# Moving the first loads and splits of the second batch earlier, in a kernel of clustered attention followed by a gated feed-forward block

## The chip, the cores and the metric

One core of one Trainium2 chip. The metric is the device time of one execution in microseconds (us). Executions can fall into a fast or a slow state. The profile and the trace are of one execution each, taken by the hardware profiler; a profiled span is some 2 us shorter than the timed execution (347.4 against 349.2 us for the kernel before).

## The reference, cut to what matters

```python
def _attn_ref(q, k, v, centroids):           # q, k, v: 4 batches x 8 heads x 768 x 64
    q_n, k_n, c_n = ...                      # each row divided by its norm
    q_assign = np.argmax(np.einsum('bhsd,hcd->bhsc', q_n, c_n), axis=-1)   # 16 clusters
    k_assign = np.argmax(np.einsum('bhsd,hcd->bhsc', k_n, c_n), axis=-1)
    mask = q_assign[:, :, :, None] == k_assign[:, :, None, :]
    scores = scale * np.matmul(q, k.transpose(0, 1, 3, 2))
    scores = np.where(mask, scores, -1000000000.0)
    ...                                      # softmax
    return np.matmul(attn, v)

def _moe_ref(x, w_gate, w_val, w_out):       # x: 3072 x 512, d_ff 1536
    gate = 1.0 / (1.0 + np.exp(-(x @ w_gate)))
    return gate * (x @ w_val) @ w_out
```

The kernel adds the mask inside the score matmul: keys and queries are split into two fp16 halves (high and low), turned so that the 64 features lie on partitions 0 to 63, and 16 "mask rows" (the one-hot cluster of each position) are placed on partitions 64 to 79.

## The kernel before: the parts that matter

Work is laid out in steps, one score matmul and one exponential each, 24 steps for a pair of heads, 96 for a batch. `at(i, f)` puts a piece of background work behind the score matmul of step i. All engines are given their instructions in this order; SyncE, which issues most of the transfers, too.

```python
    def run_bg(i):
        for f in bg.pop(i, []):
            f()
    # ... in run_steps, for each step:
                do_scores(s)
                ...
                run_bg(step_no[0])
                step_no[0] += 1
```

A pair of the batches 1 to 3 is prepared by `pair_prep`. `use` is its first step; in what follows a pair is named by it (pair 96 is the first of the second batch). The four pairs of the first batch are called 0 to 3. `load` and `hop` are transfers that SyncE issues, and a hop copies mask rows into place.

```python
    def pair_prep(b, p, use, s0, gap):
        # ...
        def ot():                             # turn the mask of the pair
            st["ot"] = ohp.tile([128, NCH, 128], HP, tag="ohT", name="ohT")
            if use == 96:
                ps = oh_turn_pe(st["oh"], NCH)
                DVE.tensor_copy(st["ot"].rearrange("p c t -> p (c t)"), ps)
            else:
                SP.dma_start_transpose(out=st["ot"], in_=st["oh"].rearrange("p c x -> p (c x)"))
        # ...
        lead = 12
        for e in range(2):                    # two heads
            s = s0 + gap * e
            at(s, lambda e=e: sp(e, 0))                       # split the keys
            at(s + gap // 2 - 1, lambda e=e: sp(e, 1))        # split the queries
            at(s + gap - 1, lambda e=e: turn((b, 2 * p + e), st["hl", e], tp))   # DMA transpose
            at(s + gap + lead, lambda e=e: lgt(e))            # logits against the centroids
            # ... the clusters are picked in the three steps after
        s = s0 + 2 * gap + lead + 4
        at(s, ot)
        s += 1 if use == 96 else 10
        at(s, lambda: hops(0))                # copy the mask rows into place
        at(s + 1, lambda: hops(1))

    for b in range(1, B):
        for p in range(NP):
            use = 96 * b + 24 * p
            first = {96: (45, 54, 5), 120: (50, 68, 8), 144: (62, 84, 10)}
            ld, s0, gap = first.get(use, (use - 76, use - 58, 10))
            for side in ("k", "q", "v"):
                at(ld, lambda b=b, p=p, side=side: load(SP, side, b, p))
            pair_prep(b, p, use, s0, gap)
```

So a load is at step `ld`, the two transposes of a pair at s0 + gap - 1 and s0 + 2 gap - 1, the logits that read them 13 steps after each.

The softmax here doesn't subtract the row's maximum and nothing guards it: scores larger than these inputs give would overflow.

## Time and profile before

| kernel before | value | how to read it |
|---|---|---|
| time | 349.66 us | median of 2 runs, 349.44 to 349.88 |
| profiled span | 347.4 us | of which TensorE busy 326.6 us (94%) |
| idle time of TensorE | 20.8 us | the span less the busy time; 16.7 of it lies before 80 us, by the sums over windows |
| step 96 (second batch begins) | 71.51 us | the 97th score matmul in the timeline |
| step 112 | 82.10 us | feed-forward matmuls are mixed in from step 104 |

What the waits and chains look like stands in the prediction below.

### The profile page before, as it was taken

The numbers are of one execution on the slowest core, as the hardware profiler recorded it, in microseconds if no ns is written. First come the engines' busy times: TensorE is split into PE (matmuls) and PEld (weight loads), VectorE is DVE, ScalarE is ACT, GpSimd is POOL, SyncE is SP. The second block draws the span as 40 slices with busy tenths as digits, with TensorE's granted clock in tenths as the row PEclk, the third lists the DMA queues.
The fourth block names the chain that finished last, engine by engine and source line by source line (L and its number), as shares of the span: only waits on it lengthen the run. The fifth ranks groups of instructions, "written<-read, shape, count | busy, mean of one in ns | idle before, by whom it ended". The sixth has DMA issues, their size and how long they took to land.

```text
span 347.4 us, 8525 instructions
## 1 busy us (share of the span) xinstructions
PE 326.6 (94%) x3274; PEld 203.9 (59%) x3274; DVE 161.2 (46%) x384; ACT 232.0 (67%) x534; POOL 134.6 (39%) x221
## 2 busy tenths in 40 slices
PE   7898783899999999999999999999999999999995
PEld 3476562556665666566666665566665665565552
DVE  6467472475653556245544455444634232242230
ACT  5687793698886788678877786588876883332321
POOL 2994584264555464515464646445220000000000
PEclk9999996599999999999999999999999999999999
DMA  7999998496965397587466397533403111200102
GB/s 223 330 198 212 251 239 208 95 229 137 173 194 111 99 221 203 111 151 191 101 185 150 113 209 172 127 90 62 87 17 103 36 22 25 90 0 32 60 0 91
DMA packets 80999, 46.43 MB, mean 134 GB/s; under 512 B 60832, under 2 KB 77888, under 8 KB 80960
## 3 DMA queue, kind: packets, MB, share of 16 engines
q1 hardware_dynamic: 76960, 40.99, 48.4%
q0 software_dynamic: 3712, 4.72, 8.0%
q8 instruction: 25, 0.41, 0.5%
q10 hardware_dynamic: 288, 0.20, 0.2%
q14 instruction: 14, 0.11, 0.1%
HBM read 28.34 MB, written 6.29 MB: 100 GB/s over the span
## 4 chain that ended last, share of the span: by engine, by line
PE 85%; DMA 7%; DVE 3%; ACT 3%; SPq 1%; issue 1%; POOL 0%; DVEq 0%
PE g L343 18%; PE v L358 18%; PE o L375 18%; PE sc L469 16%; PE av L486 9%; DMA T<-hl 3%; PE lg L275 2%; DMA qraw<-in_q_dram 2%; ACT es L474 2%; DMA T<-ohT 1%; PE t_ps L597 1%; PE lg L612 1%; PE oh_ps L325 1%; DVE hT L363 0%; PE wm L560 0%
## 5 line engine op out<-in xcount | busy, mean ns | idle before, releaser
L474 ACT ACTIVATE es<-sc 128x384 f16<-128x384 f32 x384 | 173.4, 497 | 44.0 <-PE sc L469 32.2
L469 PE MATMUL sc<-T 80*128 80x384 f16 (+1 forms) x384 | 119.2, 333 | 4.6 <-DMA T<-ohT 2.2
L486 PEld LDWEIGHTS <-es 128*128 128x128 f16 x1152 | 83.4, 99 | 46.0 <-issue 3.1
L363 DVE SCALAR_TENSOR_TENSOR hT<-th,v 128x384 f16<-128x384 f32 x96 | 53.1, 553 | 101.2 <-PE av L486 66.9
L486 PE MATMUL av<-va,es 128*128 128x65 f16 x1152 | 99.3, 195 | 0.2
L343 PE MATMUL g<-xTb,wg 128*128 128x384 f16 x384 | 78.2, 325 | 0.6 <-DVE xTb L510 0.2
L358 PE MATMUL v<-xTb,wv 128*128 128x384 f16 x384 | 78.1, 325 | 0.1
L239 POOL TENSOR_TENSOR xp<-t,rec 128x384 f16<-128x384 f32 x31 | 25.8, 831 | 129.1 <-DVE rec L238 123.1
L375 PE MATMUL o<-wo,hT 128*128 128x512 f16 x288 | 70.6, 379 | 0.0
L349 ACT ACTIVATE th<-g 128x384 f32<-128x384 f32 x96 | 47.2, 492 | 27.5 <-DVE hT L363 16.2
L343 PEld LDWEIGHTS <-wg 128*128 128x128 f16 x384 | 37.3, 97 | 22.5 <-issue 1.3
L358 PEld LDWEIGHTS <-wv 128*128 128x128 f16 x384 | 37.3, 97 | 21.1 <-issue 0.5
L375 PEld LDWEIGHTS <-hT 128*128 128x128 f16 x288 | 27.9, 97 | 25.5
L469 PEld LDWEIGHTS <-T 80*128 80x128 f16 (+1 forms) x384 | 37.6, 98 | 4.8 <-DMA T<-ohT 2.9
L384 ACT ACTIVATE ob<-o 128x512 f32<-128x512 f32 x16 | 9.6, 597 | 22.2 <-PE o L375 22.2
L237 DVE TENSOR_TENSOR t<-av,sv 128x390 f32<-128x390 f32 x32 | 18.0, 561 | 13.6 <-PE av L486 13.3
L746 POOL TENSOR_TENSOR hl<-qraw,hl 128x384 f16<-128x384 f32 x24 | 22.0, 915 | 4.8 <-DVE hl L745 3.3
L746 POOL TENSOR_TENSOR hl<-kraw,hl 128x384 f16<-128x384 f32 x24 | 22.5, 939 | 2.8 <-PE sc L469 1.2
L196 DVE TENSOR_REDUCE vs<-vraw 128x64 f16<-128x384 f32 x24 | 19.2, 814 | 0.0
L275 PE MATMUL lg<-cm,T 128*128 128x32 f16 x288 | 11.0, 177 | 8.0 <-DMA T<-hl 8.0
L281 ACT COPY lglo<-lg 128x192 f32<-128x192 f32 x24 | 7.7, 321 | 13.0 <-PE lg L275 13.0
L382 DVE TENSOR_SCALAR ob<-o 128x512 f32<-128x512 f32 x8 | 5.5, 692 | 22.8 <-PE o L375 22.8
(83 smaller groups left out, 216.6 us busy)
## 6 DMA issues: line engine op xcount, KB each, us to landing
vraw<-in_v_dram SPq DMA_DIRECT2D x16, 384.0 KB, 5.3
out_dram<-ob SPq DMA_DIRECT2D x24, 256.0 KB, 2.3
kraw<-in_k_dram SPq DMA_DIRECT2D x15, 384.0 KB, 3.5
qraw<-in_q_dram SPq DMA_DIRECT2D x15, 384.0 KB, 4.5
wg<-in_moe_w_gate_dram POOLq DMA_DIRECT2D x2, 768.0 KB, 10.3
wv<-in_moe_w_val_dram POOLq DMA_DIRECT2D x2, 768.0 KB, 13.2
wo<-in_moe_w_out_dram POOLq DMA_DIRECT2D x4, 384.0 KB, 15.3
T<-ohT SPq DMA_DIRECT2D x58, 24.0 KB, 1.9
```

What stands on the lines that cost most here:

```text
L196: DVE.tensor_reduce(s[:, e, 0:64], RAW["v", b, p][:, e].rearrange("p c d -> p d c"), AX.X, ALU.add)
L237: DVE.tensor_tensor(t, av, sv, ALU.add)
L239: eng.tensor_tensor(x, t[..., 0:64], bcast(r, 64), ALU.mult)
L343: PE.matmul(out=g[:, 0:n], lhsT=wg[fc // WQ][:, dc, fc % WQ, :], rhs=xT[:, dc, t0 : t0 + n], start=(dc == 0), stop=(dc == NDC - 1),)
L349: ACT.activation(th[:, 0:n], g[:, 0:n], AF.Tanh, scale=0.5)
L358: PE.matmul(out=w[:, 0:n], lhsT=wv[fc // WQ][:, dc, fc % WQ, :], rhs=xT[:, dc, t0 : t0 + n], start=(dc == 0), stop=(dc == NDC - 1),)
L363: DVE.scalar_tensor_tensor(hT[:, fc, 0:n], st[0][:, 0:n], 1.0, w[:, 0:n], ALU.add, ALU.mult)
L375: PE.matmul(out=o, lhsT=hT[:, fc, bass.ts(t, 128)], rhs=wo[fc // 3][:, fc % 3, :], start=(fc == 0), stop=(fc == NFC - 1),)
L469: PE.matmul(out=sc.rearrange("p (c t) -> p c t", t=128), lhsT=s["k"], rhs=s["q"], start=True, stop=True,)
L474: ACT.activation(es, sc, AF.Exp, scale=SCALE)
L486: PE.matmul(out=av[:, s["c0"] + i, :], lhsT=s["es"][:, bass.ts(i, 128)], rhs=VA[b, p][:, e, s["j"], :], start=(first and i == 0), stop=(la ...
L746: POOL.tensor_tensor(hl[:, :, 64:128], r, hl[:, :, 0:64], ALU.subtract)
```

## The change

Its intent: have the second batch's first pairs loaded, split and turned earlier, so that TensorE does not wait for their transposes around 50 to 62 us; bring the turns of the first batch's third pair forward for the same reason; and take two query casts and some warm-up matmuls off the path to the first score. The whole diff:

```diff
--- before.py
+++ after.py
@@ -512,7 +512,7 @@
         if last_x:
             at(step_no[0] + 5, by_pe)
         elif b == 0:
-            at(47 + 4 * p, by_dma)
+            at(49 + 3 * p, by_dma)
         else:
             by_dma()
 
@@ -695,14 +695,14 @@
     for e in range(2):
         split(e, 9, 12, ACT, POOL)
     k_split(1)
+    dummies(1)
+    first_pick(0)
+    first_place(0)
     for e in range(2):
         split(2 + e, 6, 12, ACT, POOL)
     load_w(0)
     dummies(3)
-    first_pick(0)
-    first_place(0)
-    dummies(3)
-    for s in range(8):
+    for s in range(4):
         at(s, lambda: dummies(1))
     for s, f in (
         (0, lambda: turn_pe([(1, 0, 6)], DVE)),
@@ -723,13 +723,13 @@
         if p > 1:
             at(U - 38, lambda p=p: k_split(p))
             at(U - 33, lambda p=p: q_split(p))
-        t_at = (8, 10, 12, 14) if p == 1 else (U - 28, U - 26, U - 24, U - 22)
-        l_at = (15, 16, 17, 18) if p == 1 else (U - 20, U - 19, U - 18, U - 17)
+        t_at = {1: (8, 10, 12, 14), 2: (19, 20, 22, 23)}.get(p, (U - 29, U - 27, U - 25, U - 23))
+        l_at = {1: (15, 16, 17, 18), 2: (25, 26, 27, 28)}.get(p, (U - 21, U - 20, U - 19, U - 18))
         for i in range(4):
             at(t_at[i], lambda x=(2 * p + i % 2, 6 * (i // 2), 6): turn_pe([x], DVE))
             at(l_at[i], lambda p=p, i=i: a_logits(p, i // 2, i % 2))
         at(l_at[3], lambda p=p: a_pick(p))
-        at(l_at[3] + (3 if p == 1 else 5), lambda p=p: a_place(p, (0,) if p == 1 else ()))
+        at(l_at[3] + (3 if p == 1 else 4), lambda p=p: a_place(p, (0,) if p == 1 else ()))
         at(U - 18, lambda p=p: v_cast(0, p))
         at(U - 5, lambda p=p: v_sum_pe(0, p))
     for i in range(4):
@@ -797,7 +797,7 @@
     for b in range(1, B):
         for p in range(NP):
             use = 96 * b + 24 * p
-            first = {96: (45, 54, 5), 120: (50, 68, 8), 144: (62, 84, 10)}
+            first = {96: (40, 46, 5), 120: (48, 60, 8), 144: (66, 84, 10)}
             ld, s0, gap = first.get(use, (use - 76, use - 58, 10))
             for side in ("k", "q", "v"):
                 at(ld, lambda b=b, p=p, side=side: load(SP, side, b, p))
```

## The prediction

> **What bounds the kernel now.** I read the page's busy slices, then the list of waits, the chain of waits in order of time, the issues of SyncE, and sums over windows of the first 72 us. The kernel walks through "steps", one score matmul (128x384) and one exponential each. Steps 0 to 95 are batch 0; from step 104 the feed-forward matmuls of the batch before are mixed in. Counting the score matmuls in the timeline gives the clock of each step: step 0 at 11.61 us, step 24 at 28.85, step 48 at 41.81, step 71 at 50.83, step 77 at 62.33, step 96 at 71.51.
>
> ```profile
> PE   7898783899999999999999999999999999999995
> ...
> PEclk9999996599999999999999999999999999999999
> DMA  7999998496965397587466397533403111200102
> ```
>
> Each digit is 8.7 us. TensorE is full from the ninth slice on. All its idle time worth having lies in the first eight, and slices seven and eight have the lower clock too. So the last 276 us (347.4 less 71.5) are fixed matmul work that this change does not touch; only the time of step 96 can move.
>
> ```profile
> PE lg L275 <- DMA T<-hl: 8.0, 2, 5.3
> ...
> PE sc L469 <- DMA T<-ohT: 2.2, 1, 2.2
> ```
>
> Waiter, what it waited for, us in total, times, longest. Three waits on transfers hold 10.2 us of TensorE: the logits of the second batch's first pair (two heads) and the mask rows of pair 2 of batch 0. The chain of waits has the same three:
>
> ```profile
> 36.97 4.71 DMA T<-ohT
> ...
> 48.59 5.23 DMA T<-hl
> ...
> 55.59 6.35 DMA T<-hl
> ```
>
> Start, length: from issue to landing. The issues of SyncE, which are in program order, show why the third is so long:
>
> ```profile
> 48.59 1.90 SPq L259 DMA_TRANSPOSE T<-hl  x1
> 50.58 3.24 SPq L329 DMA_DIRECT2D T<-ohT  x4
> 53.88 0.57 SPq L111 DMA_DIRECT2D kraw<-in_k_dram  x1
> 54.51 0.47 SPq L111 DMA_DIRECT2D qraw<-in_q_dram  x1
> 55.02 0.47 SPq L111 DMA_DIRECT2D vraw<-in_v_dram  x1
> 55.59 5.69 SPq L259 DMA_TRANSPOSE T<-hl  x2
> ```
>
> The transpose of the second head stands behind the three loads of a pair that is used 48 steps later. Now the windows (PE, PEld, DVE, ACT, POOL busy, clock, DMA share, GB/s):
>
> ```profile
> 30.00:36.00 6.00, 5.47 (x118) 4.46 (x116) 3.23 (x8) 5.37 (x13) 3.53 (x7) 1.00 1.20 212
> 36.00:41.00 5.00, 3.64 (x58) 2.86 (x56) 3.47 (x8) 4.21 (x11) 3.52 (x4) 1.00 1.23 216
> 41.00:49.00 8.00, 7.16 (x139) 5.82 (x140) 5.09 (x13) 6.54 (x16) 3.93 (x6) 1.00 1.11 332
> 49.00:54.00 5.00, 2.37 (x38) 1.73 (x35) 1.91 (x5) 3.31 (x9) 4.20 (x5) 1.00 1.13 119
> 54.00:56.00 2.00, 1.94 (x29) 1.39 (x28) 1.14 (x4) 1.56 (x4) 0.00 (x0) 0.70 0.41 85
> 56.00:64.00 8.00, 2.65 (x32) 1.71 (x30) 2.04 (x7) 2.47 (x7) 2.98 (x5) 0.50 1.10 253
> 64.00:68.00 4.00, 3.75 (x31) 2.56 (x30) 2.62 (x6) 2.93 (x7) 2.15 (x4) 0.50 0.04 10
> ```
>
> This is what carries my prediction: the DMA share is above 1 (engines full, packets queueing) without a break up to 54 us. So the wait for the first head is not merely a transfer issued too late. Everything ahead of it (the weights until 42.4, then two pairs' loads and two transposes) keeps the 16 engines full until it lands at 53.83.
>
> **What the Trainium skill says.** "DMA: Bandwidth & Descriptors", section "Issuing engines are not separate DMA queues": transfers of all issuing engines run on the same 16 DMA engines and interleave. The trace agrees: mask rows of 24 KB issued at 36.97, while GpSimd's weights ran, took 4.71 us, and rows issued after the weights take 1.9 in the median. "TensorE: Matmul & The Clock Gate", Part 1: after an idle window of about 3.4 us TensorE drops to half clock, and needs about as long a busy stretch to come back. Here the granted clock is 0.50 from 56 to 68 us, after idle times of 2.63 and 5.35 us, and 384 columns go from 0.16 us to 0.30. "Perfetto Trace Analysis", section "Tensor Engine Instruction (MATMUL, LD_WEIGHTS)": ACT, DVE and GpSimd are strictly first in, first out; so a cast that waits for a load holds what stands behind it. In this trace VectorE's first cast waited 0.6 us for its load; nothing longer shows it.
>
> **The change, part by part.**
> (a) The first placement's copy on ScalarE goes ahead of two query casts. Those wait for a load until 10.10 us and end at 11.04; the copy runs 11.07 to 11.56. But it also waits for VectorE's copy into the same tile, 10.41 to 10.96. With two warm-up matmuls fewer (0.43 us each there) the mask transposes can start at about 9.1, when VectorE's comparisons end, instead of 9.52: 0.4 to 0.5 us for step 0. The casts then lie at about 11.1 to 12.0, so the first exponential stays near 12.0.
> (b) Four warm-up matmuls fewer in steps 4 to 7: 4 x 0.22 = 0.9 us, nearly all on the path. Together (a) and (b) bring step 24 forward by up to 1.3 us, less the turns of pair 2 that now stand in VectorE's order ahead of the placement of pair 1 (one more 0.56 us copy, and a further turn that waits for a 0.62 us scaling). Near zero by step 25.
> (c) Pair 2's placement moves from step 36 to 32, and its four hops from 36.4 to about 34.2 us. At 4.7 us of flight the second lands at about 39.4, when step 48 is due. The 2.17 us wait mostly goes.
> (d) The loads of pairs 96 and 120 (named by their first step) follow the hops, so they are issued from about 36.7 instead of 38.86. The weights still hold the engines, so pair 96 lands perhaps 1 us earlier, near 42.3 (keys) and 43.3 (queries) instead of 43.34 and 44.32. VectorE reaches their casts at about 39, and stands. The turns of pair 3 wait behind it, TensorE runs dry around steps 51 to 54, and goes on near 44 us. Before, step 54 was at 44.60. So most of what (a) to (c) gained is lost again.
> (e) The logits of the first head move from step 71 to 63, those of the second from 76 to 68. Step 63 is reached at about 44 + 9 x 0.43 = 48 us (0.42 to 0.43 is ScalarE's pace: 24 exponentials in 10.14 us). The first transpose's landing: the same transfers stand ahead of it, less one attention-output transpose that is now behind it (about 2 us between its neighbours' landings), so 53.8 - 2 = 51.8, perhaps 50.5 if the transposes run closer. A wait of about 3 us stays. Then that transpose and the second head's own follow without the 144 loads: 1 to 2 us for the half-size one, 1.5 to 2 for the other, so 54 (53 to 56) instead of 61.95.
> (f) From there 28 steps to step 96, where there were 19 before. ScalarE's pace: 28 x 0.4225 = 11.8, three copies of logits 0.9, a bubble at the mask transposes as before 0.7, ten steps at the lower clock (0.485 each) 0.6: 14.0. Step 96 at 54 + 0.3 + 14.0 = 68.3 instead of 71.51.
>
> Sum: 3.2 us at step 96, all handed on to the end, less about 0.3 for new small waits for the next pair's transposes: 349.66 - 2.9 = 346.8.
>
> **The rivals.**
> 1. The waits really go. If transfers were merely issued late, the logits would find their tiles, the clock would stay up, and steps 48 to 96 would run at about 0.45 us: 2.2 + 2.6 + 5.4 us of waits and some 1 to 2 us of clock, together 11 or so: 338. For it: the named transposes are indeed issued 4 to 7 us earlier. Against it: the DMA share above 1 right up to 54 us, and the logits that need them are 8 steps earlier too.
> 2. The new wait of VectorE on the keys' load holds more than I think (pair 3's turns, its mask, step 72), and both transposes stay near 53 and 57: step 96 at 71, time 349. For it: the casts stand in front of turns in VectorE's order. Against it: a wait there is hidden under the DMA wait at step 63.
> 3. The start gets worse: with two warm-up matmuls fewer TensorE idles half a microsecond before 9.4 us, when it comes to full speed, and may stay slow for 3.4 us more. Costs 1 us at step 8, but DMA-bound steps later swallow it: 347.
>
> **Range and chances.** The second head's landing between 52 and 57 us gives step 96 between 66.3 and 71.3, that is 344.5 to 349.5; I widen the low side to 343.2 for transposes that run without pauses and a clock that stays up, and the high side to 349.9. A gain of 2% needs 342.7 or less, 7 us: rival 1 by more than half; 0.07. Slower by 2% has no mechanism in sight: 0.02.
>
> **What would show it.** In the changed profile: the wait of the score matmul for mask rows at most 0.5 us; the two waits of the logits for transposes still in the list, the first about 3 us and the second under 2, instead of 2.6 and 5.3; a new wait of VectorE's casts on the loads of keys and queries of 1 to 4 us; DMA share above 1 until about 54 us; half clock for a shorter stretch than 13.7 us; the first 80-row score matmul (step 96) near 68 us; everything after it as long as before. I am wrong if the first logits wait is gone (transfers not bound by the engines' rate), or if step 96 comes before 65 or after 71 us.

## More of the kernel before

Pairs from 168 on take the general rule: the loads of pair 168 are at step 168 - 76 = 92.

One more view of the kernel before is needed later: SyncE's issues from 70 to 79 us (start, duration, line, what). The load at 70.25 is the first of the three of pair 168, the transpose at 71.98 is the first of pair 144, and `ohT<-oh` at 77.36 is the mask of pair 120.

```profile
70.25 0.57 SPq L111 DMA_DIRECT2D kraw<-in_k_dram  x1
...
71.98 3.03 SPq L259 DMA_TRANSPOSE T<-hl  x1
77.36 2.01 SPq L771 DMA_TRANSPOSE ohT<-oh  x1
```

## The result, and the profile after

The changed kernel takes 354.91 us (median of 2 runs, 354.69 to 355.14), 1.5% more than before: ratio 1.015, 95% interval 1.011 to 1.019. Ratios here and below are the mean time of one kernel's fast runs over that of the kernel before in the same rounds, so they are not quite the ratios of the medians quoted. The prediction was 346.8 us with a range of 343.2 to 349.9; it was wrong, and in the sign.

The busy slices of the changed kernel, each 8.83 us (353.3 / 40):

```profile
PE   7896778767999999999999999999999999999995
...
PEclk9999988896999999999999999999999999999999
```

The dip that stood in slice seven before (3 busy tenths) has filled up (8), as meant. A new one stands in slices nine and ten (6 and 7, that is 70.7 to 88.3 us), and the clock of slice ten is 6 tenths. TensorE's waits of over 1.5 us from 40 us on, from its timeline (start, duration, instruction, and in brackets the idle time before it and what ended that):

```profile
44.57 0.45 PE L612 MATMUL lg<-cm,T 128*128 128x16 f16 x12 [2.69 <-DVE T L598]
...
52.89 0.47 PE L275 MATMUL lg<-cm,T 128*128 128x32 f16 x12 [1.78 <-DMA T<-hl]
...
63.55 0.49 PE L275 MATMUL lg<-cm,T 128*128 128x32 f16 x12 [1.84 <-DMA T<-hl]
...
81.88 0.50 PE L275 MATMUL lg<-cm,T 128*128 128x32 f16 x12 [5.16 <-DMA T<-hl]
```

The first two are in the prediction (turns held behind casts that wait for loads; the first head's transpose), the third with too small a size. The last was not in it: the logits of pair 144, at step 106, wait 5.16 us for their transpose. The chain of waits has it as its longest piece, 8.04 us from issue to landing:

```profile
70.38 0.50 POOL oh L763
...
72.16 0.57 SPq L111
...
73.80 8.04 DMA T<-hl
```

And SyncE's issues tell what stands ahead of it. The same part of the queue as shown for the kernel before, now of the changed one:

```profile
64.01 1.27 SPq L501 DMA_TRANSPOSE xTb<-xp  x1
70.89 1.21 SPq L771 DMA_TRANSPOSE ohT<-oh  x1
72.16 0.57 SPq L111 DMA_DIRECT2D kraw<-in_k_dram  x1
...
73.80 2.23 SPq L259 DMA_TRANSPOSE T<-hl  x1
```

SyncE issued nothing from 65.28 to 70.89 us. It stood at the transpose of pair 120's mask, whose last piece GpSimd finished at 70.88 (the first line of the chain above: 70.38 + 0.50). Behind it stood three loads that waited for nothing, and behind those the transpose that TensorE needed (its own data had been split by 70.00). Before, the loads and the transpose came first (70.25 and 71.98) and the mask after them (77.36). The change brought pair 120's splits from step 68 to 60, so its mask transpose moved from step 68 + 32 = 100 to 60 + 32 = 92; the loads of pair 168 are at step 92 too and the transpose of pair 144 at step 93. In the same step the piece that was registered first is issued first, and pair 120 is registered before pair 168.

Three windows of the changed kernel (PE, PEld, DVE, ACT, POOL busy, clock, DMA share, GB/s):

```profile
66.00:72.00 6.00, 5.61 (x77) 3.60 (x75) 3.97 (x13) 5.92 (x16) 4.52 (x6) 0.91 0.13 12
76.00:82.00 6.00, 0.84 (x11) 0.52 (x10) 1.12 (x2) 0.98 (x2) 0.00 (x0) 0.89 1.13 180
82.00:88.00 6.00, 6.00 (x44) 3.39 (x44) 2.32 (x7) 3.19 (x7) 0.62 (x1) 0.54 0.77 240
```

From 66 to 72 us the DMA engines are 13% busy, moving 12 GB/s, for want of issues. From 76 to 82 they are full and TensorE has nothing to do. And from 82 to 88 TensorE is full again at about half clock: 44 matmuls where an undisturbed version, shown below, makes 69.

Counting score matmuls in the timelines gives the clock of each step. Where the time is won and lost:

| step | before, us | after, us | difference |
|---|---|---|---|
| 0 | 11.61 | 10.79 | -0.82 |
| 24 | 28.85 | 29.06 | +0.21 |
| 48 | 41.81 | 40.37 | -1.44 |
| 60 | 46.73 | 49.90 | +3.17 |
| 78 | 62.79 | 60.53 | -2.26 |
| 96 | 71.51 | 70.07 | -1.44 |
| 106 | 77.66 | 75.65 | -2.01 |
| 108 | 79.12 | 82.68 | +3.56 |
| 112 | 82.10 | 88.00 | +5.90 |
| 383 (last) | 288.66 | 294.63 | +5.97 |

Up to step 106 the change is 2.0 us ahead. Two steps later it is 3.6 behind (5.6 lost, 5.16 of it the wait), four further steps cost 2.3 more at half clock, and after step 112 nothing changes any more.

### The profile page after: what moved, and what is told of

It reads as the page before. It is cut to its first block, busy times and chain, and to the rows that moved or that the text cites.

```text
span 353.3 us, 8515 instructions
## 1 busy us (share of the span) xinstructions
PE 328.5 (93%) x3268; PEld 204.7 (58%) x3268; DVE 161.2 (46%) x384; ACT 232.3 (66%) x534; POOL 134.6 (38%) x221
## 3 DMA queue, kind: packets, MB, share of 16 engines
q0 software_dynamic: 3712, 4.72, 7.8%
## 4 chain that ended last, share of the span: by engine, by line
PE 83%; DMA 10%; DVE 4%; issue 1%; ACT 1%; SPq 1%; POOL 0%; DVEq 0%; ACTq 0%
PE v L358 18%; PE g L343 18%; PE o L375 18%; PE sc L469 15%; PE av L486 8%; DMA T<-hl 6%; PE lg L275 2%; DMA kraw<-in_k_dram 2%; DMA T<-ohT 2%; PE wm L560 1%; PE t_ps L597 1%; DVE T L598 1%; DVE oh L293 1%; DVE hT L363 0%; DVE T L631 0%
## 5 line engine op out<-in xcount | busy, mean ns | idle before, releaser
L469 PE MATMUL sc<-T 80*128 80x384 f16 (+1 forms) x384 | 120.7, 337 | 2.1 <-DMA T<-ohT 1.4
L358 PE MATMUL v<-xTb,wv 128*128 128x384 f16 x384 | 79.0, 328 | 0.1
L304 DVE TENSOR_TENSOR lgs<-lg,lglo 128x192 f32<-128x192 f32 x24 | 8.2, 343 | 17.3 <-ACT lglo L281 16.9
```

The lines of the kernel that those rows point to most:

```text
L358: PE.matmul(out=w[:, 0:n], lhsT=wv[fc // WQ][:, dc, fc % WQ, :], rhs=xT[:, dc, t0 : t0 + n], start=(dc == 0), stop=(dc == NDC - 1),)
L469: PE.matmul(out=sc.rearrange("p (c t) -> p c t", t=128), lhsT=s["k"], rhs=s["q"], start=True, stop=True,)
```

## The experiments

Theory A, from the profile: the blocked queue. The mask transpose at step 92 holds up the loads and the transpose behind it. Rival B: the DMA engines are simply fuller, since the loads of pair 144 moved as well (62 to 66). Rival C: TensorE now comes to step 106 two microseconds earlier, and would have waited for that transpose anyway, since before it landed at 78.1 (71.98 and 6.1 us of flight), just when step 106 came (77.66).

| run | what | us, median | ratio to before | 95% interval |
|---|---|---|---|---|
| the change | | 354.91 | 1.015 | 1.011 to 1.019 |
| e1 | mask of pair 120 two steps later | 347.3 | 0.9926 | 0.991 to 0.995 |
| e9 | loads of pair 168 one step earlier | 347.36 | 0.9923 | 0.988 to 0.997 |
| e4 | pair 120's splits back at 68 | 347.84 | 0.995 | 0.992 to 0.998 |
| e5 | before, with pairs 120 and 144 moved | 355.01 | 1.015 | 1.013 to 1.017 |
| e3 | before, with pair 96 alone moved | 350.69 | 1.0022 | 0.9995 to 1.005 |
| g1 | before, with the start alone changed | 349.85 | 1.0009 | 0.995 to 1.007 |
| e7 | e1, turns of pairs 2 and 3 back | 347.9 | 0.9932 | 0.989 to 0.998 |
| e6 | e1, output weights loaded later | 345.8 | 0.9881 | 0.983 to 0.993 |
| e6 again | | 346.01 | 0.9912 | 0.989 to 0.994 |
| b3 | before, output weights loaded later | 350.91 | 1.0047 | 1.002 to 1.007 |
| b1 | e6, pair 96 loaded at step 28 | 346.61 | 0.9911 | 0.988 to 0.994 |
| b2 | b1, output transposes later | 346.92 | 0.9922 | 0.989 to 0.996 |

All gave correct results.

**e1: the mask transpose out of the way.** One line in the changed kernel:

```diff
         s = s0 + 2 * gap + lead + 4
+        s += 2 if use == 120 else 0
         at(s, ot)
```

> The changed kernel, but with the transpose of the mask of pair 120 put two steps later, from step 92 to 94, so that in SyncE's order it stands behind the loads of pair 168 and the first transpose of pair 144 instead of ahead of them. Theory A (the blocked queue): the loads go out near 65 us instead of 72.2, that transpose lands near 75 to 77 instead of 81.8, the 5.2 us wait at step 106 shrinks to under 1 us, the half clock after it goes too, total 346.5 to 348.5. Rival B (the DMA engines are just fuller, since the loads of pair 144 were also moved): transpose still lands after 80 us, total 353 or more. Rival C (TensorE now comes to step 106 2 us earlier and would have waited anyway): a wait of 2 to 3 us stays, total 350 to 351.

Measured: 347.3 us, so 7.6 us below the changed kernel and 0.7% below the kernel before. SyncE's issues and the window that was empty:

```profile
65.31 1.24 SPq L111 DMA_DIRECT2D kraw<-in_k_dram  x1
...
69.30 2.01 SPq L259 DMA_TRANSPOSE T<-hl  x1
71.43 1.21 SPq L771 DMA_TRANSPOSE ohT<-oh  x1
```

```profile
66.00:72.00 6.00, 4.34 (x67) 2.77 (x64) 3.74 (x11) 5.23 (x15) 4.57 (x6) 1.00 0.91 246
...
76.00:82.00 6.00, 6.00 (x70) 3.99 (x68) 3.88 (x10) 5.12 (x13) 1.81 (x4) 1.00 0.86 151
82.00:88.00 6.00, 6.00 (x69) 3.98 (x68) 3.23 (x9) 4.83 (x13) 2.87 (x5) 1.00 0.60 168
```

The loads leave at 65.31 instead of 72.16, the engines are 91% busy from 66 to 72, and TensorE is full at full clock from 76 us on. Step 106 comes at 75.53 and step 108 at 77.00: no wait. This is what theory A asked for, with its numbers. B asked for 353 or more and C for 350 to 351.

**e9: which half of the block does the harm.** In the changed kernel:

```diff
             ld, s0, gap = first.get(use, (use - 76, use - 58, 10))
+            ld = 91 if use == 168 else ld
```

> The changed kernel with the loads of pair 168 one step earlier, 91 instead of 92: they now stand ahead of the blocked mask transpose in SyncE's order, while the first transpose of pair 144 stays behind it. This tells apart the two ways the block can hurt. If the harm is that the three loads start late and the transpose then queues behind them in the DMA engines: loads out near 65 us, the transpose issued near 72 lands near 75 to 76, wait at step 106 under 1 us, total 346.5 to 348.5. If the harm is that the transpose's own issue is held until the mask is ready: it still lands near 79 or later, a wait of 3 us or more, total 350 to 354.

Measured: 347.36 us. The loads are now ahead of the mask, the transpose still behind it:

```profile
64.94 1.51 SPq L111 DMA_DIRECT2D kraw<-in_k_dram  x1
...
70.30 1.23 SPq L771 DMA_TRANSPOSE ohT<-oh  x1
71.59 1.45 SPq L259 DMA_TRANSPOSE T<-hl  x1
```

The transpose, issued at 71.59, took 3.3 us to land and was there in time (step 106 at 75.38, 108 at 76.84). In the changed kernel it was issued 2.2 us later (73.80) and took 8.04. So of the 7 us by which it came late, 4.7 (8.04 less 3.3) are the flight behind three loads that had been issued just ahead of it. Of the 2.2 us of later issue, 1.6 are the time that SyncE took to issue these loads (72.16 to 73.80) and 0.6 a mask that was ready later (70.89 against 70.30). The loads that nobody was in need of did the greater harm.

**e4: pair 120 back alone.** In the changed kernel:

```diff
-            first = {96: (40, 46, 5), 120: (48, 60, 8), 144: (66, 84, 10)}
+            first = {96: (40, 46, 5), 120: (48, 68, 8), 144: (66, 84, 10)}
```

> The changed kernel with the splits of pair 120 alone set back, from step 60 to 68 (its mask transpose then falls to step 100, behind the others again). Theory A: as in the run with the mask transpose later, 346.5 to 349, no wait of over 1 us at step 106. Rival B: 353 or more, for the loads of pair 144 stay at step 66. Rival C: 350 to 351.

Measured: 347.84 us, step 106 at 75.29 and 108 at 76.75. The loads of pair 144 stay at step 66 here, so B falls; TensorE comes to step 106 as early as in the changed kernel, so C in its full size falls. A wait of 2.78 us for pair 120's first transpose, at step 88, is new here.

**e5: the harmful part alone, put into the kernel before.**

```diff
-            first = {96: (45, 54, 5), 120: (50, 68, 8), 144: (62, 84, 10)}
+            first = {96: (45, 54, 5), 120: (48, 60, 8), 144: (66, 84, 10)}
```

> The kernel before with the numbers of pairs 120 and 144 of the change alone (loads at 48 and 66, splits of pair 120 from step 60); the first pair as before. Theory A: the block at step 92 comes back: the loads of pair 168 stand behind the mask transpose, a wait of 4 to 6 us at step 106 and half clock after it. The second head's transpose, now ahead of the loads of pair 144, gives some 3 to 4 us back earlier, so total 351 to 355. Rival C (only the earlier arrival exposes the transpose): with the first pair as before the wait at step 106 is under 2 us and the total 347 to 350.

Measured: 355.01 us. The mask transpose issues at 71.76, the loads at 73.06, and TensorE's timeline has the wait:

```profile
82.50 0.50 PE L275 MATMUL lg<-cm,T 128*128 128x32 f16 x12 [4.98 <-DMA T<-hl]
```

Step 78 was 4.3 us earlier than before (58.47 against 62.79), since the second head's transpose now stands ahead of the loads of pair 144. By step 112 it was 6.7 us behind (88.81 against 82.10). So these two entries of the table alone make the slowdown. They also free the second head, by the later loads of pair 144. It is the entry of pair 120 that does the harm, since e4 keeps the loads at 66 and is not slow.

**e3: pair 96 alone moved, in the kernel before.**

```diff
-            first = {96: (45, 54, 5), 120: (50, 68, 8), 144: (62, 84, 10)}
+            first = {96: (40, 46, 5), 120: (50, 68, 8), 144: (62, 84, 10)}
```

> The kernel before with one part of the change alone: the loads of the second batch's first pair at step 40 instead of 45, its splits from step 46 instead of 54. Pairs 120 and 144 as before. Theory A: this part is good: second head's transpose lands near 55 instead of 61.95, step 96 one to three us earlier, no new wait at step 106 beyond 1 us, total 347 to 348.5. Rivals B and C: B says no harm either (loads of 144 not moved), C says a wait of 1.5 to 3 us at step 106 since its transpose landed at 78.1 before, total 349.5 to 350.5.

Measured: 350.69 us, ratio 1.0022: the same as before, a miss of mine by 2 us. Both early logits waits fell from 2.63 and 5.35 to one of 4.50, and at step 88 the kernel was 2.3 us ahead (66.33 against 68.59). Then a new wait took it:

```profile
69.05 0.47 PE L275 MATMUL lg<-cm,T 128*128 128x32 f16 x12 [2.30 <-DMA T<-hl]
```

These are pair 120's logits at step 88. With pair 96 earlier, its mask rows (step 73) are issued ahead of pair 120's first transpose (step 75); before, the transpose came first. That this order makes the wait is argued, not tested. e4, with pair 120's splits at the same step, has the wait too and is still faster than before. The time is near the one that C had named, but not by C's wait: there is none at step 106 (78.53, step 108 at 80.00). In e3 the start was also 0.8 us behind by step 4 (15.84 against 15.00), with the clock at half from 11.4 to 14.8 us in the profiled run; the start is the same program as before.

**g1 and e7: the other parts of the change.** g1 is the kernel before with the first placement ahead of the query casts and six warm-up matmuls fewer:

```diff
     k_split(1)
+    dummies(1)
+    first_pick(0)
+    first_place(0)
     for e in range(2):
         split(2 + e, 6, 12, ACT, POOL)
     load_w(0)
     dummies(3)
-    first_pick(0)
-    first_place(0)
-    dummies(3)
-    for s in range(8):
+    for s in range(4):
```

> The kernel before with the change of the start alone: first placement ahead of the query casts, six warm-up matmuls fewer. Steps 0 and 8 come 0.8 to 1.6 us earlier; but the first head's transpose is bound by the DMA engines at 53.8 us and the second by the loads ahead of it, so that at step 77 nearly nothing is left: total 348.8 to 350, ratio 0.997 to 1.0. If the start counts in full: 348.

Measured: 349.85 us, ratio 1.0009. It is 1.49 us ahead at step 8 and 1.29 at step 24, and 0.44 us behind at step 78. A wait for mask rows of 1.21 us at step 36 took part of the lead (0.68 us was left at step 48), and 1.3 us went between steps 48 and 54 (41.13 to 45.22, against 41.81 to 44.60 before), since TensorE ran at half clock from 41.98 to 45.40 after a wait of 2.09 us. The kernel before had waited 2.17 us there and kept its clock, so this part of the loss may be chance. The two logits waits stayed as long (2.70 and 5.08).

e7 is e1 with the turns, logits and placements of pairs 2 and 3 at their old steps:

```diff
-        t_at = {1: (8, 10, 12, 14), 2: (19, 20, 22, 23)}.get(p, (U - 29, U - 27, U - 25, U - 23))
-        l_at = {1: (15, 16, 17, 18), 2: (25, 26, 27, 28)}.get(p, (U - 21, U - 20, U - 19, U - 18))
+        t_at = (8, 10, 12, 14) if p == 1 else (U - 28, U - 26, U - 24, U - 22)
+        l_at = (15, 16, 17, 18) if p == 1 else (U - 20, U - 19, U - 18, U - 17)
...
-        at(l_at[3] + (3 if p == 1 else 4), lambda p=p: a_place(p, (0,) if p == 1 else ()))
+        at(l_at[3] + (3 if p == 1 else 5), lambda p=p: a_place(p, (0,) if p == 1 else ()))
```

> The version with the mask transpose at step 94, but with the turns, logits and placements of pairs 2 and 3 at their old steps. My reading is that part (c) gives nearly nothing: in the version with the earlier turns two waits of 1.8 and 1.5 us (VectorE's mask copy ahead of a turn, and the mask rows of pair 1 at step 36) take the place of the 2.2 us at step 48. So the total is within 1 us of that version: 346.5 to 348.3. If the earlier turns matter (author's intent): 1.5 to 2.5 us slower, 349 to 350.

Measured: 347.9 us, against 347.3 with the earlier turns; the intervals overlap. Part (c) of the change is worth nothing that stands out: with the old turns TensorE waits 2.44 us at step 48, with the new ones 1.78 us at step 23 and, in e1, 1.54 at step 36.

**e6 and b3: is the first transpose bound by the engines' rate?** The prediction leaned on it. In e1, and in the kernel before, the loads of the output weights (first used near 102 us) were moved:

```diff
     for i in range(4):
-        at(9 + 5 * i, lambda i=i: load_wo(i))
+        at(108 + 5 * i, lambda i=i: load_wo(i))
```

> The version with the mask transpose at step 94, and the four output weights' loads (first used near 103 us) moved from steps 9 to 24 to steps 108 to 123. It tests the step of the prediction which says that the DMA engines' rate, not the time of issue, sets the first head's transpose. If the rate sets it: without 5 to 6 us of weight traffic the loads of pair 96 land near 39 instead of 43.6, the first transpose near 47 to 49 instead of 52.8, the waits at steps 51 and 63 go (2.3 and 1.3 us), step 96 comes 2 to 4 us earlier, total 343 to 345.5 if the late weights do not get in the way. If the order of issue sets it: transpose lands after 51 us and the total is 346.5 to 348.

> The kernel before with the output weights' loads alone moved from steps 9 to 24 to steps 108 to 123. If the weights' traffic is what holds the first pair's loads and the mask rows of pair 2: the 2.2 us wait at step 48 falls under 0.5, the first head's transpose lands 2 to 3 us earlier than 53.8; the second stays behind the loads of pair 144 and gains no more than the same. Total 346.5 to 348.5. If the order of SyncE's issues is all: 349 to 350.

Measured: 345.8 us for e6, the fastest of all, and 350.91 for b3, slower than before by 0.5%. In e6 the DMA engines were 27% busy from 34 to 38 us, where they had been full. The wait for mask rows is gone: in b3 from step 48 (2.17 us before), in e6 from step 36 (1.54 in e1). But in e6 the first head's logits still waited, now 4.72 us, until 50.94 instead of 52.83 in e1. SyncE's issues in e6:

```profile
39.25 1.86 SPq L501 DMA_TRANSPOSE xTb<-xp  x1
41.98 5.29 SPq L259 DMA_TRANSPOSE T<-hl  x1
```

The transpose is offered at 41.98 and takes 5.29 us to issue, with pair 120's loads and an output transpose queued ahead of it. So the truth lies between my two readings: without the weights the transpose comes 1.9 us earlier, not the 4 to 6 us that I expected. What is queued directly ahead of it matters too: in b1 below, with these loads and the output transposes behind it (and pair 96 loaded earlier too), it landed at 45.2. In b3 the first head's logits came at 52.38 instead of 53.87. TensorE came to step 106 at 75.72, 1.9 us earlier than before, and waited there:

```profile
78.20 0.46 PE L275 MATMUL lg<-cm,T 128*128 128x32 f16 x12 [1.41 <-DMA T<-hl]
```

So the old order of the queue brings that transpose just in time for the old pace. This is rival C, and it is real, at 1.4 us. It does not show in e1, e4 or e9, where pair 120's second transpose stands earlier and the loads of pair 168 leave between 64.9 and 66.2 us instead of at 70.25. The trace is of b3's fastest execution (349.07 us), so what made its median longer than before is not shown. e6 was run again with more rounds:

> The fastest version so far (mask transpose of pair 120 at step 94, output weights' loads at steps 108 to 123) once more, with more rounds, to see whether its 345.8 us holds: expected 345 to 346.7, ratio 0.986 to 0.991. If it falls together with the version that only moves the mask transpose (347.3), moving the weights gave nothing that stands out of the spread.

Measured: 346.01 us, ratio 0.9912 (0.989 to 0.994). The median holds, the ratio is nearer to that of e1 and e9 than expected, and the intervals overlap. So e6 beats the kernel before by about 1%, and that the later weights add to it is likely from the trace (step 112 at 78.11 against 79.98 in e1) but not shown by the times.

**b1 and b2: two attempts at more.** In e6:

```diff
-            first = {96: (40, 46, 5), 120: (48, 60, 8), 144: (66, 84, 10)}
+            first = {96: (28, 44, 5), 120: (48, 60, 8), 144: (66, 84, 10)}
```

and for b2 `(28, 44, 5)`, `(49, 62, 8)` and, for the output transposes, `at(56 + 3 * p, by_dma)`.

> The version with the mask transpose at step 94 and the late output weights, and in addition the loads of pair 96 at step 28, ahead of pair 2's mask rows, its splits from step 44, so that its first transpose stands ahead of pair 120's loads in SyncE's order. In the version without this it was issued at 42.0, took 5.3 us to issue and landed at 50.9 behind those loads, though the DMA engines stood nearly idle from 34 to 37.5 us. Expected if the order in the queue is what is left: first transpose lands near 43 to 45, the wait of 4.7 us at step 63 goes, the second lands near 49 to 51 with a wait of 1 to 3 us: total 342 to 344.5. If the splits (VectorE, GpSimd) or the transposes themselves set it: 345 to 346.

> As the run before it, with both attention-output transposes of batch 0 moved from steps 49 and 52 to 56 and 59, behind the second head's transpose, and pair 120's loads and splits one and two steps later. Expected: second head's transpose lands 1 to 2 us earlier than there, total the same to 1.5 us faster, 341 to 344; worse by up to 1 us if pair 120's later splits make its own transposes late at step 82.

Measured: 346.61 and 346.92 us, no better than e6. In b1 the first transpose was issued at 41.44 and landed 3.8 us later, 45.2: its wait was gone, as expected. The second head took it over:

```profile
53.69 0.50 PE L275 MATMUL lg<-cm,T 128*128 128x32 f16 x12 [5.12 <-DMA T<-hl]
```

Pair 120's loads and both output transposes stood ahead of it. In b2 the output transposes did not, yet it waited 5.19 us and TensorE went on at 53.44. What holds the second transpose at 53 us in b2 is not settled; pair 120's three loads, issued from 43.77 on, still stand ahead of it in both.

## Why the prediction was wrong

**The step that failed.** "So the last 276 us (347.4 less 71.5) are fixed matmul work that this change does not touch; only the time of step 96 can move." The loss lies between step 106 and step 112. Of the signs that it named, "everything after it as long as before" is the one whose failure made the loss. Two smaller ones failed as well: a wait for mask rows of 1.43 us stood at step 36 where at most 0.5 was said, and the second wait of the logits was gone instead of under 2 us. The sum took the busy share of TensorE after 80 us as proof that nothing there could come to wait. But that share only says that before, everything arrived in time. It says nothing of how closely. The first transpose of pair 144 came just in time (landed at 78.1, its logits began at 78.57), and what issues it is a queue that the change reordered.

**What was overlooked in it.** Moving `s0` of pair 120 from 68 to 60 moves not only its splits and its two transposes, but everything counted from them: the mask transpose from step 100 to 92. Parts (d) and (e) went through the splits and the transposes, and never asked what the mask transpose would meet at step 92. It met the loads of pair 168. The runs showed in its place: SyncE at a standstill from 65.28 to 70.89 us, the engines 13% busy meanwhile, a wait of 5.16 us at step 106, and 2.3 us more at half clock. e1 and e9 take it away with one line each; e5 makes it with one line.

**(a) and (b), the start.** Right within the spread. Step 0 came 0.82 us earlier (0.4 to 0.5 said), step 8 by 1.6, and at step 24 nothing was left (+0.21). Single traces are a rough measure here: with the same start as the changed kernel, e1, e4 and e9 reach step 24 between 28.65 and 30.47 us. g1, without the turns of pair 2, was still 1.29 us ahead at step 24 (up to 1.3 said).

**(c), pair 2's mask rows.** Right in its part: the wait at step 48 went. The 1.78 us at step 23 are the loss by the turns of pair 2 that (b) had reckoned with, in kind. Not foreseen were the 1.43 us at step 36. The part as a whole gave nothing that stands out (e7).

**(d), VectorE held by loads.** Right: its cast waited 3.41 us for the keys (1 to 4 said), which landed at 43.6 instead of my 42.3, and TensorE waited 2.69 us for the turn behind it and went on at 44.57 (near 44 said).

**(e), the two transposes.** About right: the first head's logits began at 52.89 (51.8 said), after a wait of 1.78 us (about 3 said); the second's transpose landed at 54.8 (54 said) and was no longer waited for. The reason that I gave for the first, the engines' rate, was only part of it: without the output weights it came 1.9 us earlier (e6).

**(f), to step 96.** 70.07 us where 68.3 was said, inside the 66.3 to 71.3 given. The second head's logits came at 56.10 instead of 54, although their transpose had landed: TensorE reached step 68 only then, at half clock from 53.39 on. From there to step 96 it took 13.97 us, where 14.0 was said. That agreement is partly luck, since a wait of 1.84 us at step 80 lies in it, where 0.3 was allowed for all such waits.

**The versions without the block** took 347.3 and 347.36 us against the 346.8 predicted for the change. So the total was good for the work that the sum looked at, in part by luck: they reached step 96 at 69.95 and 69.80 us, not at 68.3. Rival 1 (all waits go, 338) and rival 2 (nothing gained, 349) were both further off; a rival in which an issue queue blocks was missing from the list.

## What to carry to other kernels

When a piece of work is moved, list everything whose time is counted from it, and read the order of every queue that it goes through, to the end of the program. In an in-order issue queue like SyncE's here, a transfer that waits for late data must not stand ahead of loads that wait for nothing: the loads start late, and then delay the transfer that is needed next. A fully busy engine after some point is no proof of slack there: ask by how much each transfer came in time.

## What the Trainium skill lacked or had wrong

- "DMA: Bandwidth & Descriptors", section "Queues, rings and completion order", says that each DMA engine goes round the queue rows for which it has work, packet by packet. While GpSimd's weight loads ran, 24 KB of mask rows issued by SyncE took 4.7 us in the kernel before and, in the changed one, 6.2 us (issued at 29.38), against 1.9 in the median. A short transfer beside a deep queue of another engine was not quick; the section gives no time for this case.
- The same page, section "Issuing engines are not separate DMA queues", calls the issuing sequencer's time usually small next to the transfer. For DMA transposes it was not: one of 128 x 1536 fp16 elements took SyncE between 1.43 us of 4.9 to landing (at 62.49 in the changed kernel) and 5.29 us of 8.9 (e6, with loads queued ahead). All issues behind it wait as long.
- "Perfetto Trace Analysis", section "DMA Instruction — HWDGE (DVE, Sync)", puts the wait for the semaphores of a transfer into the sequencer that issues it, which is free for the next instruction only after the issue. No page read draws the consequence that decided here: an issue that waits for its data holds loads behind it that wait for nothing. It left the engines 13% busy for 6 us and cost 7.6 us in all (354.91 against 347.3 us).
- "TensorE: Matmul & The Clock Gate", Part 1, puts the drop to half clock after an idle window of about 3.4 us. Waits of 2.69 us (at 44.57) and 1.84 us (at 63.55) were also followed by stretches at half clock, as these windows of the changed kernel show (clock is the third figure from the right). The length of one wait does not settle it: at step 48, 2.17 us left the kernel before at full clock and 2.09 us were followed by half clock in g1.

```profile
47.00:50.00 3.00, 2.84 (x27) 2.00 (x25) 2.05 (x5) 1.98 (x5) 3.00 (x5) 0.50 1.34 157
...
64.00:66.50 2.50, 2.50 (x23) 1.58 (x20) 2.03 (x6) 2.36 (x6) 0.18 (x1) 0.50 1.48 187
```
